# Splitting a sequence's attention jobs at a unit boundary, and storing the last result by halves

## The chip, the cores and the metric

The kernel runs on one core of one Trainium2 chip. The metric is the device time of the whole kernel in microseconds. Five engines run side by side, each in its own program order: TensorE (PE, with its weight loads shown as PEld), VectorE (DVE), ScalarE (ACT), GpSimd (POOL) and SyncE (SP), which issues most of the DMA transfers.

## The reference

```
scores = q @ k^T / 8;  ret = scores * gamma_h ** (i - j) for i >= j, else 0
x = (ret @ v), heads side by side            # 8 sequences of 576 tokens, 8 heads of 64 -> 4608 x 512
xn = x / sqrt(mean(x*x) + 1e-6) * rms_g
out = (silu(xn @ w_gate) * (xn @ w_val)) @ w_out     # 512 -> 1536 -> 512
```

Everything is float32, except that gate's, value's and the output's weights arrive as 64-bit floats and are brought to 32 bits in the kernel.

## The kernel before

**Attention.** A job is one sequence `b` and one pair of heads `hp`, so there are 8 x 4 = 32 jobs, numbered in that order. A job has nine chunks of 64 tokens (`NC` = 9, `L` = 64). Within a chunk the product is taken directly (`scores`, then `weigh` by the decay and the causal mask, then `values`), and what earlier chunks hand on goes through a running 64 x 64 state per head (`states` on PE, `sums` on DVE, `carried` on PE). The moves at the end of `carried` (L397, DVE) put the result into the token-feature tile `x`. One call of `slot(j)` issues `values(j-1)`, `scores(j)`, `states(j)`, `weigh(j)`, `carried(j-1)` and `sums(j)`. `carried` may start only after a small write to `tick` that follows `values`.

**Units.** The feed-forward part takes 12 units of 384 tokens (`U`; `HU` = 192 is half). Three units cover two sequences: units 0 and 1 hold all 576 tokens of the first sequence and the first 192 of the second; unit 2 is the other 384 tokens of the second.

**Opening.** Units 0 and 1 are treated apart. First all eight jobs of the first two sequences run, one `slot` after the other. Their q and k are turned by matmuls against an identity (`turn`, evicted by ACT, L239 and L248), and their v is scaled by ACT (`scale_v`, L264). Between slots DVE and ACT begin to round the weights: there are 18 chunks of 64-bit weights, and each takes the DVE operations L811 (exponent), L838, L843 (mantissa), L848 (sign) and L856 (join), with three ACT operations L827 between L811 and L848. The words of a chunk are loaded into one of four places, and a load that waits for a place is issued from ACT's queue right behind the L848 which frees it (L795).

**Gate's and value's products of units 0 and 1** (`up_plain`, L614) follow. They are issued in 48 equal steps: for each of three groups of columns, gate (m = 0) and then value (m = 1), for each of two units, four steps. I number these steps 0 to 47; steps 24 to 31 and 40 to 47 are value's in the second and third group. One step is four matmuls of 128x384 into one PSUM bank, followed by its eviction: ACT with a silu for gate (L622), DVE with a multiplication for value (L620). After each step the program queues two more pieces of weight rounding (`weights(2)`) and one ACT piece (`act(1)`). PE's results of steps, `values`, the last state of a job (`last`) and the turned q and k all come from one pool of five PSUM banks.

**After that** the output products of units 1 and 0 run (`across`, L688), while DVE combines the weights (L652, L672), and units 2 to 11 follow in one steady form, in which products are formed from sums and differences of blocks (L557, L564). Here the remaining jobs, from number 8 on, are spread over the units: `load_next` fetches q, k and v by DMA two jobs ahead, `prepare` turns q and k by DVE transposes (L255), and `slot` runs the job between two products.

The order on each engine is the program's (`manual_schedule`), so an instruction that waits holds up all that is queued behind it on its engine.

Of the kernel before, what the change touches and what calls it, by code (L numbers as in the profile page):

```python
# [14 lines left out]
P = 128  # L15
# [26 lines left out]
def kernel(  # L42
# [88 lines left out]
    jobs = [(b, hp) for b in range(B) for hp in range(NHP)]  # L131
# [4 lines left out]

    def load_qk(j):
        b, hp = jobs[j]
        for nm, src in (("q", q), ("k", k)):

            t = raw.tile([P, S // SQ, SQ], F32, tag=nm + "raw", name=f"{nm}raw_{j}")
            for e in range(2):
                rows = src[b, 2 * hp + e].rearrange("(t b) (i a) -> i b t a", b=SQ, a=SQ)
                for i in range(D // SQ):
                    r = e * D + i * SQ
                    nc.sync.dma_start(out=t[r : r + SQ], in_=rows[i])
            st[j][nm + "raw"] = t

    def load_first(j, tails):

        b, hp = jobs[j]
        d = st[j]
        room = h_of[0].rearrange("p f t -> p (f t)")
        part = room[:, j * 4 * P : j * 4 * P + 4 * P]
        d["q"] = part.rearrange("p (e t d) -> p e t d", e=2, d=D)
        nc.sync.dma_start(
            out=part.rearrange("p (e t) -> p e t", e=2),
            in_=q[b, 2 * hp : 2 * hp + 2, : NFULL * P].rearrange("e (p t) d -> p e (t d)", p=P),  # L160
        )
        for nm, src in (("k", k), ("v", v)):
            t = d[nm] = first_places[nm][j].rearrange("p (c e d) -> p c e d", e=2, d=D)
            for e in range(2):
                nc.sync.dma_start(
                    out=t[:, :, e],
                    in_=src[b, 2 * hp + e, : NFULL * P].rearrange("(c p) d -> p c d", p=P),
                )
            for n in (0, 1) if nm == "k" else (2,):
                load_tails(b, n, tails)  # L170
# [33 lines left out]
    def load_kv(j):  # L204

        b, hp = jobs[j]
        for nm, src, bufs in (("k", k, 4), ("v", v, 3)):
            t = raw.tile([P, NFULL, 2, D], F32, tag=nm, name=f"{nm}_{j}", bufs=bufs)
            for e in range(2):
                nc.sync.dma_start(  # L210
                    out=t[:, :, e],
                    in_=src[b, 2 * hp + e, : NFULL * P].rearrange("(c p) d -> p c d", p=P),
                )
            st[j][nm] = t
        t = st[j]["vt"] = raw.tile([L, 2, D], F32, tag="vt", name=f"vt_{j}", bufs=3)
        nc.sync.dma_start(
            out=t, in_=v[b, 2 * hp : 2 * hp + 2, NFULL * P :].rearrange("e p d -> p e d")
        )

    def turn(j):  # L220

        d = st[j]
        last = bank(f"turn_{j}_t")
        for nm in "qk":
            ps = bank(f"turn_{j}_{nm}")
            for c in range(NFULL):
                if nm == "k":
                    nc.tensor.transpose(
                        out=ps[:, c * P : c * P + P],
                        in_=d["k"][:, c].rearrange("p e d -> p (e d)"), identity=ident,  # L230
                    )
                    continue
                for e in range(2):
                    nc.tensor.matmul(
                        ps[side(e), c::NFULL], lhsT=d["q"][:, e, c], rhs=ident,
                        start=True, stop=True,
                    )
            t = d[nm + "T"] = att.tile([P, S], F32, tag=nm + "T", name=f"{nm}T_{j}")
            nc.scalar.copy(out=t[:, : NFULL * P], in_=ps)  # L239
        for i, nm in enumerate("qk"):  # L240
            o = slice(i * TAIL, i * TAIL + TAIL)
            nc.tensor.transpose(
                out=last[:, o], in_=d[nm + "t"].rearrange("p e d -> p (e d)"),
                identity=ident[:TAIL, :TAIL],
            )
        for i, nm in enumerate("qk"):
            o = slice(i * TAIL, i * TAIL + TAIL)
            nc.scalar.copy(out=d[nm + "T"][:, NFULL * P :], in_=last[:, o])  # L248

    def prepare(j):  # L250

        d = st[j]
        for nm in ("q", "k"):
            t = att.tile([P, S], F32, tag=nm + "T", name=f"{nm}T_{j}")
            nc.vector.transpose(out=t, in_=d.pop(nm + "raw").rearrange("p t a -> p (t a)"))  # L255
            d[nm + "T"] = t
        scale_v(j)

    def scale_v(j):
        d = st[j]  # L260
        hp = jobs[j][1]
        for e in range(2):
            for t in (d["v"][:, :, e], d["vt"][:, e]):
                nc.scalar.activation(  # L264
                    out=t, in_=t, func=AF.Copy, scale=gv[: t.shape[0], hp, e : e + 1]
                )
# [9 lines left out]
    def scores(j):  # L276

        d = st[j]
        s = d["s"] = trio.tile([P, 3, 512], F32, tag="s", name=f"s_{j}")
        for c in range(NC + 1):  # L280
            i, odd = divmod(c, 2)
            c = min(c, NC - 1)
            for e in range(2):
                nc.tensor.matmul(  # L284
                    s[side(odd), e, i * L : i * L + L], lhsT=d["kT"][side(e), c * L : c * L + L],
                    rhs=d["qT"][side(e), c * L : c * L + L], start=True, stop=True,
                )
# [8 lines left out]
    def states(j):  # L296

        d = st[j]
        d["last"] = bank(f"last_{j}")
        for c in range(NC - 1):  # L300
# [8 lines left out]
    def weigh(j):  # L309

        d = st[j]
        hp = jobs[j][1]
        s = d["s"]
        ret = d["ret"] = att.tile([P, 2, NFULL + 1, L], F32, tag="ret", name=f"ret_{j}", bufs=1)
        for e in range(2):
            nc.vector.scalar_tensor_tensor(
                out=ret[:, e], in0=s[:, e, :SC].rearrange("p (c k) -> p c k", k=L),
                scalar=float(_gamma(H)[2 * hp + e] ** -L),
                in1=causal.unsqueeze(1).to_broadcast([P, NFULL + 1, L]),
# [3 lines left out]
    def sums(j):  # L323

        d = st[j]
        hp = jobs[j][1]
        t = d["sum"] = att.tile([P, NC - 1, L], F32, tag="sum", name=f"sum_{j}")
        for c in range(NC - 1):
            part = state_of(d, c)
            if c == 0:  # L330
                nc.vector.tensor_copy(out=t[:, 0], in_=part)
                continue
            nc.vector.scalar_tensor_tensor(  # L333
                out=t[:, c], in0=t[:, c - 1], scalar=gc[:, hp : hp + 1], in1=part,
                op0=ALU.mult, op1=ALU.add,
            )
        del d["s"], d["last"]
# [10 lines left out]
    def values(j):  # L348

        d = st[j]  # L350
        av = d["av"] = [bank(f"av_{j}_{i}") for i in range(2)]
        for c in range(NC):
            i, odd = divmod(c, 2)
            for e in range(2):
# [4 lines left out]
                    start=(c < 2), stop=False, skip_group_check=True,  # L359
# [3 lines left out]
        if j == 2 * NHP:  # L363
# [5 lines left out]
    def carried(j):  # L369

        d = st[j]
        b, hp = jobs[j]
        av = d["av"]
        for c in range(1, NC):
            i, odd = divmod(c, 2)
            for e in range(2):
                mm = nc.tensor.matmul(  # L377
                    av[odd][column(j, odd, e), i * L : i * L + L], lhsT=d["sum"][side(e), c - 1],
                    rhs=d["qT"][side(e), c * L : c * L + L],
                    start=False, stop=(c >= NC - 2), skip_group_check=True,  # L380
                )
                if c == 1 and e == 0:
                    follow(mm, d["valued"])
        for c0, c1 in ((0, 2 * HU), (2 * HU, S)) if b % 2 == 0 else ((0, HU), (HU, S)):
# [289 lines left out]
    def across(u):  # L674
# [8 lines left out]
        def product(rhs, ps, start):  # L683
            k = 7 * (u - 2) + n_done
            a = first_blocks[ORDER[n_done]] if u < 2 else w_slots[:, k % 4]
            for i in range(2):
                for c in range(NH):
# [4 lines left out]
                    )  # L692
            if u > 1 and n_done < 3:
# [8 lines left out]
        def result(row, col, a, ps):  # L702
# [5 lines left out]
            end = u == NU - 1  # L708
            if not end:
                nc.vector.transpose(out=o, in_=r)  # L710
            o_of = o.rearrange("p (d t r) -> p d t r", d=2, r=SQ)
            for d in range(2):
                if end:
                    half = slice(d * HU, d * HU + HU)
                    nc.vector.transpose(out=o[:, half], in_=r[:, half])
                for i in range(P // SQ):
                    c0 = row * DH + d * P + i * SQ
                    t0 = u * U + col * HU
                    queue = nc.scalar if end and i % 2 else nc.sync
                    queue.dma_start(  # L720
                        out=out[t0 : t0 + HU, c0 : c0 + SQ].rearrange("(t c) r -> c t r", c=SQ),
                        in_=o_of[i * SQ : i * SQ + SQ, d],
                    )
# [31 lines left out]
        product(b21, w, False)  # L755
        result(1, 0, u2, w)
# [134 lines left out]
    steps = rounding()  # L891

# [12 lines left out]
    def start():  # L905
# [20 lines left out]
        for j in range(2 * NHP):  # L926
            load_first(j, {0: range(2), 1: range(2, H), NHP: range(H)}.get(j))
# [9 lines left out]
        squares = []  # L937
        for j in range(2 * NHP):
# [24 lines left out]
        made = combine_out()  # L963
        for m, g in [(m, g) for g in range(NG) for m in range(2)]:
            for u in range(2):
                weights_to(4 * g + 2 * m + 1)
                for i, _ in enumerate(up_plain(u, m, g)):
                    if not (u or m or g):
# [23 lines left out]
        following(2 * NHP - 1)  # L992
# [12 lines left out]
        slot(8, rest=False)  # L1005
        following(8)
# [3 lines left out]
        slot(9)  # L1010
        following(9)
# [7 lines left out]
    def behind(u, i):  # L1019
        at, n = SLOTS[u % 3]  # L1020
        if i in at:
            j = u // 3 * 8 + n + at.index(i)
# [7 lines left out]
    with tc.manual_schedule():  # L1030
# [4 lines left out]
        for u in range(2, NU):  # L1035
# [11 lines left out]
            for i, _ in enumerate(rest):  # L1047
                if i == 0 and turns:
                    prepare_next(turns.pop())
                if i == 2:  # L1050
                    behind(u, 6)
                    at, n = SLOTS[u % 3]
                    if 2 * NG - 1 in at:
                        load_next(u // 3 * 8 + n + len(at) - 1)
# [31 lines left out]
```

## Time and profile before

| what | value |
|---|---|
| median of 3 runs | 1143.16 us (1141.73 to 1143.99) |
| span of the profiled run | 1141.5 us |
| PE busy | 1119.3 us, 98% |
| DVE busy | 726.9 us, 64% |
| ACT busy | 258.7 us, 23% |
| granted TensorE clock, mean | 0.995 |
| opening, until the first gate product | 0 to 61.7 us |
| the 48 steps | 61.7 to 191.0 us |
| output products of units 1 and 0 | 191.0 to 248.3 us |

A busy PE in this table is one that has an instruction running; the stage decides whether that instruction waits for anything. The stages are read from the chain of waits, which lists in order of time the pieces of work that the end of the run goes back to.

### The profile page before, as it was taken

What the parts mean: (1) busy time and instruction counts of PE and PEld (TensorE: products, weight loads), DVE (VectorE), ACT (ScalarE), POOL (GpSimd) and SP (SyncE); (2) the same over time, 40 slices, a digit from 0 to 9 for tenths busy, and PEclk for the clock granted to TensorE, in tenths of its full rate; (3) what the DMA queues carried; (4) which work ended last, traced back from release to release, by engine and by line L of the source; (5) the groups of instructions that cost most, each with busy time, mean ns of one, the idle gap of its engine ahead of it and who ended that gap; (6) DMA issues with size and microseconds to landing.
All of it is one profiled execution on the core that took longest, in us unless ns stands there. A gap on an engine that the chain in (4) does not pass through costs nothing.

```text
span 1141.5 us, 24713 instructions
## 1 busy us (share of the span) xinstructions
PE 1119.3 (98%) x10470; PEld 1046.5 (92%) x10470; DVE 726.9 (64%) x1431; ACT 258.7 (23%) x508; POOL 39.5 (3%) x64
## 2 busy tenths in 40 slices
PE   8889999999999999999999999999999999999998
PEld 6655557999999999999999999999999999999998
DVE  5788877745685685375767676466577566446352
ACT  5545642002211221111221121121121220120210
POOL 0000000370000000000000000000000000000000
PEclk8999999999999999999999999999999999999999
DMA  8765326335463465044444555306436403303304
GB/s 205 208 157 175 113 102 211 62 67 127 110 131 76 139 149 155 1 109 100 100 125 67 122 140 121 115 30 121 107 89 143 131 32 96 127 1 99 124 1 111
DMA packets 292943, 125.40 MB, mean 110 GB/s; under 512 B 270433, under 2 KB 275809, under 8 KB 292833
## 3 DMA queue, kind: packets, MB, share of 16 engines
q1 hardware_dynamic: 282688, 107.66, 38.3%
q10 hardware_dynamic: 10144, 16.16, 4.4%
q8 instruction: 82, 1.34, 0.5%
q14 instruction: 29, 0.23, 0.1%
HBM read 108.83 MB, written 14.94 MB: 108 GB/s over the span
## 4 chain that ended last, share of the span: by engine, by line
PE 93%; DVE 3%; issue 1%; DMA 1%; ACT 1%; SPq 0%; DVEq 0%; POOLq 0%; POOL 0%; ACTq 0%
PE w L557 13%; PE x L557 13%; PE z L557 13%; PE up L614 11%; PE xo L688 8%; PE wo L688 8%; PE zo L688 8%; PE y L557 6%; PE yo L688 4%; PE av L355 2%; PE av L377 2%; PE s L284 2%; PE s L304 1%; DVE x L397 1%; DVE sum L333 1%
## 5 line engine op out<-in xcount | busy, mean ns | idle before, releaser
L581 ACT COPY m<-x 128x384 f32<-128x384 f32 x60 | 28.7, 478 | 338.3 <-PE x L557 338.3
L688 PE MATMUL xo<-h,w_out 128*128 128x192 f32 x528 | 90.3, 328 | 0.0
L557 PE MATMUL w<-sums,w_val 128*128 128x192 f32 x480 | 88.6, 328 | 0.4
L557 PE MATMUL x<-x,w_val 128*128 128x192 f32 x480 | 88.8, 328 | 0.0
L557 PE MATMUL z<-x,w_gate 128*128 128x192 f32 x480 | 87.9, 326 | 0.7 <-DVE u L564 0.7
L557 PE MATMUL x<-x,w_gate 128*128 128x192 f32 x480 | 88.5, 328 | 0.0
L557 PE MATMUL w<-sums,w_gate 128*128 128x192 f32 x480 | 87.8, 326 | 0.0
L557 PE MATMUL z<-x,w_val 128*128 128x192 f32 x480 | 87.8, 326 | 0.0
L688 PEld LDWEIGHTS xo<-h,w_out 128*128 128x128 f32 x528 | 85.9, 190 | 0.6
L688 PE MATMUL wo<-h,w_out 128*128 128x192 f32 x504 | 85.3, 326 | 0.0
L564 DVE TENSOR_TENSOR u<-m,y 128x384 f32<-128x384 f32 x60 | 33.1, 552 | 79.1 <-PE y L557 79.1
L688 PEld LDWEIGHTS wo<-h,w_out 128*128 128x128 f32 x504 | 82.5, 190 | 0.0
L557 PEld LDWEIGHTS w<-sums,w_val 128*128 128x128 f32 x480 | 79.2, 190 | 2.7 <-DVE c L564 2.7
L557 PEld LDWEIGHTS z<-x,w_gate 128*128 128x128 f32 x480 | 79.6, 190 | 1.0 <-issue 1.0
L557 PEld LDWEIGHTS x<-x,w_val 128*128 128x128 f32 x480 | 79.2, 190 | 0.6
L557 PEld LDWEIGHTS x<-x,w_gate 128*128 128x128 f32 x480 | 79.3, 190 | 0.5
L557 PEld LDWEIGHTS z<-x,w_val 128*128 128x128 f32 x480 | 79.7, 190 | 0.0
L557 PEld LDWEIGHTS w<-sums,w_gate 128*128 128x128 f32 x480 | 79.6, 190 | 0.0
L564 DVE TENSOR_TENSOR h<-u,w 128x384 f32<-128x384 f32 x60 | 33.0, 550 | 69.5 <-PE w L557 69.4
L576 ACT ACTIVATE h<-h 128x384 f32<-128x384 f32 x90 | 47.0, 523 | 89.5 <-DVE h L564 89.5
L614 PE MATMUL up<-x,w_gate 128*128 128x384 f32 x192 | 63.3, 488 | 0.9 <-DVE x L526 0.7
L614 PE MATMUL up<-x,w_val 128*128 128x384 f32 x192 | 62.7, 487 | 0.0
(187 smaller groups left out, 1770.6 us busy)
## 6 DMA issues: line engine op xcount, KB each, us to landing
w_out<-w_blocks SPq DMA_DIRECT2D x70, 768.0 KB, 5.1
out_dram<-o SPq DMA_DIRECT2D x368, 24.0 KB, 1.6
qraw<-in_q_dram SPq DMA_DIRECT2D x96, 72.0 KB, 2.9
kraw<-in_k_dram SPq DMA_DIRECT2D x96, 72.0 KB, 3.0
k<-in_k_dram SPq DMA_DIRECT2D x48, 128.0 KB, 3.0
v<-in_v_dram SPq DMA_DIRECT2D x48, 128.0 KB, 3.1
w_out<-in_moe_w_gate_dram ACTq DMA_DIRECT2D x5, 1024.0 KB, 5.9
w_out<-in_moe_w_out_dram ACTq DMA_DIRECT2D x3, 1024.0 KB, 4.9
```

The source lines that it names most:

```text
L284: nc.tensor.matmul(s[side(odd), e, i * L : i * L + L], lhsT=d["kT"][side(e), c * L : c * L + L], rhs=d["qT"][side(e), c * L : c * L + L], ...
L304: nc.tensor.matmul(o[side(e)], lhsT=d["k"][side(odd), i, e], rhs=d["v"][side(odd), i, e], start=True, stop=True,)
L333: nc.vector.scalar_tensor_tensor(out=t[:, c], in0=t[:, c - 1], scalar=gc[:, hp : hp + 1], in1=part, op0=ALU.mult, op1=ALU.add,)
L355: mm = nc.tensor.matmul(av[odd][column(j, odd, e), i * L : i * L + L], lhsT=d["v"][side(odd), i, e] if c < NC - 1 else d["vt"][:, e], rhs= ...
L377: mm = nc.tensor.matmul(av[odd][column(j, odd, e), i * L : i * L + L], lhsT=d["sum"][side(e), c - 1], rhs=d["qT"][side(e), c * L : c * L + L],
L397: nc.vector.tensor_tensor(out=x[to, first - c0 // L :: 2], in0=av[odd][at, i * L : (i + n) * L].rearrange("p (c k) -> p c k", k=L), in1=g. ...
L557: nc.tensor.matmul(ps[:, i * HU : i * HU + HU], lhsT=w_up[m][:, 2 * blk + c, cut], rhs=t_of[u][blk][:, c], start=(start and i == c == 0), ...
L564: nc.vector.tensor_tensor(out=o, in0=a, in1=pairs_of(ps), op=ALU.add)
L576: nc.scalar.activation(out=o, in_=c, func=AF.Silu)
L581: nc.scalar.copy(out=s1, in_=pairs_of(x_))
L614: nc.tensor.matmul(ps[:, :U], lhsT=w_up[m][:, 4 * half + c, i * P : i * P + P], rhs=x_of[u][:, c], start=(c == 0), stop=(c == NHP - 1),)
L688: nc.tensor.matmul(ps[:, i * HU : i * HU + HU], lhsT=a[:, c, i * P : i * P + P], rhs=rhs[:, c], start=(start and i == c == 0), stop=False, ...
```

## The change

The jobs of the second sequence are cut at its token 192, where unit 2 begins. Only the first three chunks of those four jobs stay in the opening, since units 0 and 1 need no more. The other six chunks become four jobs of their own (numbers 8 to 11), which are loaded, prepared and run among the 48 steps of gate's and value's products. The state that a first part hands to its second part is kept in unit 2's tile `x`, in a place that the second part overwrites last. All later jobs keep their places and get numbers that are four higher.

Two smaller things change besides. The transposes of the third later job (`prepare`) are no longer queued right before unit 2, but within its first block of products. And the last result of the last unit is made by halves: once the first half's products are done, its sum, transpose and stores are issued, and the second half's products follow; before, one sum was taken over both halves after all products.

```diff
-    jobs = [(b, hp) for b in range(B) for hp in range(NHP)]
+    CUT = HU // L
+    parts = [(0, 0, NC), (1, 0, CUT), (1, CUT, NC)] + [(b, 0, NC) for b in range(2, B)]
+    jobs = [(b, hp, c0, c1) for b, c0, c1 in parts for hp in range(NHP)]
+    LATER_JOBS = 3 * NHP
...
+    LATER_AT = (29, 33, 37, 41, 45)
...
+        def later(step):
+
+            if step == LATER_AT[0] - 8:
+                following(2 * NHP - 1)
+            elif step in LATER_AT:
+                j = 2 * NHP + LATER_AT.index(step)
+                if j < LATER_JOBS:
+                    slot(j, rest=(j > 2 * NHP))
+                    if j + 1 < LATER_JOBS:
+                        following(j)
+                else:
+                    values(j - 1)
+                    carried(j - 1)
...
                 for i, _ in enumerate(up_plain(u, m, g)):
+                    step += 1
+                    later(step)
...
         combine(0)
-        slot(9)
-        following(9)
+        slot(LATER_JOBS + 1)
+        load_next(LATER_JOBS + 1)
+        turns.append(LATER_JOBS + 1)
...
+        def last_result(d):
+
+            if not d:
+                o = outs.tile([P, DM], F32, tag="o", name="o_last")
+                halves.extend((temp("c_last"), o))
+            r, o = halves
+            nc.vector.tensor_tensor(
+                out=r[:, half(d)], in0=u2[:, half(d)], in1=w[:, half(d)], op=ALU.add
+            )
+            nc.vector.transpose(out=o[:, half(d)], in_=r[:, half(d)])
+            store(o, 1, 0, d)
...
-        product(b21, w, False)
-        result(1, 0, u2, w)
+        if u == NU - 1:
+            product(b21, w, False, last_result)
+        else:
+            product(b21, w, False)
+            result(1, 0, u2, w)
```

`following(j)` is `prepare(j + 1)` and the load of job `j + 2`. So at step 21 job 8 is prepared and job 9 loaded; at steps 29, 33, 37 and 41 the slots of jobs 8 to 11 run, each with the next one's preparation but for the last; at step 45 `values` and `carried` of job 11 close the series. The rest of the diff carries the bounds of a job's chunks through loads, turns, scores, states, sums and moves.

## The prediction

> **What bounds the kernel now.** I read the page, then the chain of waits, stage by stage, then the timelines of DVE, ACT and the weight loads where the moved work will land. All times are us; step s is the s-th of the 48 product steps.
>
> ```profile
> PE   8889999999999999999999999999999999999998
> DVE  5788877745685685375767676466577566446352
> ```
>
> Of the page's 40 slices (28.5 us each) only the first three leave PE idle; everything later is PE work. So the opening can lose idle time, and what is moved into the steps is paid for at PE's price.
>
> The chain of waits in the opening, from the fifth job's slot on:
>
> ```profile
> 41.31 0.93 PE av L355 x36
> 42.23 0.58 PE s L284 x40
> ...
> 44.02 0.93 PE av L377 x31
> 44.95 1.05 PE turn_q L234 x16
> 46.02 0.59 ACT qT L239
> 46.61 0.58 ACT kT L239
> ...
> 58.90 2.18 issue
> ...
> 61.70 2.78 PE up L614 x8
> ...
> 76.88 100.89 PE up L614 x312
> ```
>
> A slot is a ring of PE work and two ACT evictions, about 5.2 long, with stretches called issue in between (0.89, 2.06, 0.40, 0.81 and 2.18 from 30.8 on). DVE is nearly as long. Its timeline in the slots of jobs 4 to 7 has 0.89 for weighing, 2.35 for the sums, 0.95 for the moves, and 0.55 to 2.2 for squares, norm and weight rounding each. Step 0 starts at 61.70, step 4 at 76.88, and then a step is 8 x 0.324 = 2.59 until 190.97 without a gap.
>
> In the steps, the end of the weight rounding on DVE:
>
> ```profile
> 169.25 1.22 DVE L848 SCALAR_TENSOR_TENSOR w_gate<-w_gate 128x1024 uint32<-128x1024 uint32 x1
> 175.50 0.70 DVE L811 TENSOR_SCALAR w_gate<-w_gate 128x1024 uint32<-128x1024 uint32 x1 [5.03 <-DMA w_gate<-in_moe_w_out_dram]
> ...
> 180.24 1.23 DVE L848 SCALAR_TENSOR_TENSOR w_gate<-w_gate 128x1024 uint32<-128x1024 uint32 x1 [1.04 <-ACT w_gate L827]
> 181.39 0.54 DVE L620 TENSOR_TENSOR h<-h,up 128x384 f32<-128x384 f32 x1
> ```
>
> The L848 of chunk 16 frees the place of chunk 17, whose load takes 5.0; the L811 of chunk 17 waits for it, and the evictions are queued behind. The L620 at 181.39 evicts step 40, which PE ended at 76.88 + 37 x 2.59 = 172.8, 8.6 earlier. ACT is held in the same way:
>
> ```profile
> 176.23 1.15 ACT L827 ACTIVATE w_gate<-w_gate,least 128x1024 f32<-128x1024 uint32 x1 [9.01 <-DVE w_gate L811]
> 177.28 0.47 ACT L622 ACTIVATE w_val<-up 128x384 f32<-128x384 f32 x1
> ```
>
> That L622 evicts step 38. And the weight loads:
>
> ```profile
> 177.80 12.55 PEld L614 LDWEIGHTS up<-x,w_val 128*128 128x128 f32 x40 [0.65 <-ACT w_val L622]
> ```
>
> Step 43 takes the bank of step 38, five back: PE already runs its five banks out here and waits for nothing only because it is just in time.
>
> [...]queue q8 has 82 packets and 1.34 MB, 16.3 KB each, and PE resumes after the issue stretches at 31.7, 37.9, 43.3 and 49.6, some 126 matmuls (252 instructions) apart. [...]So loads of the moved jobs delay chunk loads; in the opening, where both run, a chunk takes 5.9 in the median against 4.9 for the w_out chunks on ACT's queue. [...]weighing, which needs the scores alone, starts after the states in neighbouring columns (DVE ret L316 waits for PE s L304). [...]
>
> **The change part by part.**
>
> *Opening.* Up to the turn of job 4 (30.1) nothing changes. DVE is busy without a break to the L811 at 33.99 to 34.69, so the weighing of job 4 starts at 34.7 (before: 35.7). From there DVE sets the pace. A half slot costs it 2 x 0.245 for weighing 128 columns (0.445 for 320, at 1.05 ns a column by 0.55 for 384 and 1.22 for 1024), 0.21 + 2 x 0.31 for sums and 0.29 + 0.21 for two moves instead of four: 1.83 against 4.2. Slot 4 still moves job 3 (0.94) and has two squares (1.1) and L838 (0.69): to 38.8. Slot 5: 1.83, r 0.16, L843 1.22, then it waits for the power on POOL (1.65) and forms the diagonals (0.68): to 43.3. Slot 6: 1.83, norm 2.19, L848 1.22: to 48.6. Slot 7: 1.83 and two squares 1.2: to 51.65. PE, about 2.2 a half slot, stays beside this[...]. Step 0 begins when the first norm column is there, at 45.9, ends at 48.5, waits for the weighing of job 7 (49.1), and its moves end at 52.15, against 67.63. Square and sum 1.1, L811 0.69 and L856 1.22 follow, to 55.1; before, 69.99. Step 2 needs that L856, so all later steps are **14.9 earlier**.
>
> *PE's work in the steps.* Full slots in units 2 and 3 take 0.67 values, 0.58 scores, 0.39 states, 0.50 carried and 0.2 of switching. Of that 6/9, 8/10, 5/8 and 6/8: 1.7 for a later job. Five calls, 0.7 + 3 x 1.7 + 1.2 (the last with nothing to hide tick), are 7.0.
>
> *DVE's work in the steps.* A later job costs 0.76 weighing, 5 x 0.31 sums, 1.07 moves (0.35 and 2 x 0.36), 1.10 transposes (0.77 and 0.735 for 576 columns, less 192 x 1.05 ns each). I follow chunk 17's L811, before at 175.50:
> - Step 29 puts 3.4 (no moves yet) ahead of chunk 13's L848. DVE has 0.16 idle there: +3.3, and the load behind it is later by as much.
> - Step 33 puts 4.5 between chunk 14's L848 and the next L811, where DVE idled 3.9 for a load: +0.6.
> - Step 37 puts 4.5 ahead of chunk 16's L848, whose load everything waits for: +4.5.
> - The loads of jobs 10 and 12 are issued beside two of those chunk loads. By 5.9 against 4.9 I take +0.6 each, +1.2; nothing at best, 1.5 each at worst.
>
> Together +9.6 (8.4 to 11.4): L811 at 185.1 on the old clock. Queued behind it, and thus late: on ACT the evictions of steps 38 and 39, on DVE those of 40 to 43. PE waits for their banks. The slot at step 41 takes three banks (two av, one last), so step 42 now needs step 40's bank. Before, step 45 did. From L811 to the end of that eviction is 181.9 - 175.5 = 6.4; then steps 42 to 47 (6 x 2.59) and the last call (1.2): the steps end 23.2 after L811, against 191.0 - 175.5 = 15.5 before. So **+7.7 + 9.6 = 17.3**; 7.0 of it is PE's own work and the rest waiting. An earlier wait at step 35 (about 3, ACT held by the load behind chunk 14's L848) lies inside this. The transposes at step 21 cost nothing: by step 27 DVE waited 0.52 for PE before. ACT's v scaling, tick's memset on POOL and the load of job 8 lie beside PE's products.
>
> *Unit 2.* PE waits 0.70 at 257.2 for a DVE sum behind the transposes; with these queued later: **-0.7**.
>
> *The end.* Before: sum 0.57, two half transposes, four stores of 0.43 per queue, the last issued at 1138.8. After: sum 0.35, transpose 0.33, two stores per queue, 1.1 sooner. If PE may not write the bank meanwhile, it waits about 0.5 for the first half's sum: **-0.8** (0.6 to 1.1).
>
> Sum: -14.9 + 17.3 - 0.7 - 0.8 = +0.9; 1143.16 + 0.9 = **1144.1**.
>
> **The rivals.**
> - *Hidden.* The jobs' DVE work falls into DVE's 13.4 of waiting (3.4, 3.9, 5.0 and 1.0 from 150 to 180), and PE pays 7.0 and a wait of some 4: -14.9 + 11 - 1.5 = -5.4, 1137.8; with no wait 1133.8. For it: the idle time is there. Against it: two of the three insertions before L811 come just before an L848 that starts a load, so the idle time moves with them.
> - *More contention.* Chunk loads at the worst value (+1.8), and the opening 3 less[...]: 1144.1 + 4.8 = 1148.9, slower. For it: DMA is 79% busy from 30 to 62. Against it: DVE, not DMA, set the pace there.
>
> **How the numbers follow.** An even trade (1141 to 1147): 0.48. Hidden (1133 to 1141): 0.31. Contention (1147 to 1153): 0.21. The bound of 0.2% is 2.3, so faster means under 1140.9, slower over 1145.4. The even trade is spread over that bound: 0.02 of it faster, 0.34 same, 0.12 slower. So faster 0.33, same 0.34, slower 0.33. The range cuts off 1 in 10 at each end: 1136.0 to 1149.5.
>
> **What would show it.** Step 0 near 46 and step 4 near 62 (opening); a wait of several us at the weight loads or av of the slot at step 41 and at step 42, for ACT w_val L622 and DVE h L620; chunk 17's L811 some 9.6 later against step 31 than before; steps ending near 193.4. If PE runs through steps 35 to 47 with waits under 3 in all, I am wrong and Hidden is right; if step 4 starts after 65, the opening's sum is wrong.

## The result and the profile after

| | before | after |
|---|---|---|
| median of 6 runs each | 1141.89 us (1139.81 to 1143.99) | 1148.47 us (1146.38 to 1149.55) |
| ratio after / before | | 1.0056, 95% interval 1.0041 to 1.0072 |
| span of the profiled run | 1141.5 us | 1147.0 us |
| step 4 starts | 76.88 | 62.47 |
| exponent of chunk 17 starts | 175.50 | 172.72 |
| the steps end | 190.97 | 198.91 |

The change makes the kernel slower, by 6.6 us in the medians and 5.5 in the profiled pair. The forecast was 0.9 slower. The median lies in the band that the forecast gave to *More contention*, not in that of its even trade.

In the new numbering of lines the product steps are L652, their evictions L660 (ACT) and L658 (DVE). Of the weight rounding, the exponent is L871, the sign L908, ACT's operations L887, and the load behind the sign L855. `weigh` is L342, the moves L435, the transposes of `prepare` L272, `values` L390, `carried` L412 and the write to `tick` L401.

The page's slices of the changed kernel, the ones shown of before:

```profile
PE   7899988999999999999999999999999999999998
DVE  5888777747586586466766776466577576446353
```

The third slice reads 9 where it read 8, and step 4 starts 14.4 sooner: the opening did get shorter. The sixth and seventh slice, from 143 to 201 us, fell from 9 to 8: PE now waits there. Which waits these are, the chain of waits shows. From step 4 on it reads (start, length, what):

```profile
62.47 67.35 PE up L652 x208
...
130.75 0.76 DVE ret L342 x2
...
136.29 1.15 DVE w_gate L908
137.46 6.60 DMA w_out<-in_moe_w_out_dram
144.16 0.69 DVE w_gate L871
...
147.85 0.67 DVE ret L342 x2
148.53 0.36 DVE x L435
...
149.40 9.67 PE up L652 x24
...
164.63 1.12 DVE w_gate L908
165.78 6.92 DMA w_gate<-in_moe_w_out_dram
172.72 0.70 DVE w_gate L871
...
179.20 12.95 PE up L652 x32
```

Before, PE's products were one piece of 100.89 from step 4 on. Now the chain leaves PE at step 29 (129.8) and goes through DVE: weighing, the sign of chunk 13, the load which that sign releases, the exponent of chunk 15, weighing again, and back to PE for one stretch; then the same once more through chunks 16 and 17. The loop that the forecast describes, slot to sign to load to exponent to eviction, is there line by line. PE's three longest waits between 62 and 200 (us in total, times, longest):

```profile
PE up L652 <- DVE x L435: 3.6, 1, 3.6
PE av L390 <- ACT w_val L660: 3.5, 1, 3.5
PE up L652 <- DVE h L658: 1.3, 1, 1.3
```

The first is step 35, whose bank waits for slot 9's moves; the second is the slot of step 41, the third step 42. These are the places and the releasers of the forecast. DVE's and ACT's timelines around chunk 17:

```profile
164.56 1.18 DVE L908 SCALAR_TENSOR_TENSOR w_gate<-w_gate 128x1024 uint32<-128x1024 uint32 x1
172.72 0.69 DVE L871 TENSOR_SCALAR w_gate<-w_gate 128x1024 uint32<-128x1024 uint32 x1 [6.98 <-DMA w_gate<-in_moe_w_out_dram]
```

```profile
173.45 1.15 ACT L887 ACTIVATE w_gate<-w_gate,least 128x1024 f32<-128x1024 uint32 x1 [10.58 <-DVE w_gate L871]
174.50 0.47 ACT L660 ACTIVATE w_val<-up 128x384 f32<-128x384 f32 x1
```

DVE idles 6.98 for chunk 17 (5.03 before), and ACT 10.58 behind it (9.01). The L660 at 174.50 is the eviction that the slot of step 41 waits for.

What the forecast doesn't have is in the windows around the two long pauses, of step 35 and step 41 (us, busy time and count of PE, PEld, DVE, ACT, POOL, then the granted clock, the DMA share and GB/s):

```profile
151.00:153.00 2.00, 2.00 (x5) 1.09 (x4) 2.00 (x4) 2.00 (x3) 0.00 (x0) 0.50 0.71 250
173.00:175.00 2.00, 0.00 (x0) 0.00 (x0) 2.00 (x3) 1.55 (x3) 0.00 (x0) 0.69 1.23 208
175.00:177.00 2.00, 1.98 (x72) 1.98 (x76) 1.38 (x2) 2.00 (x3) 0.09 (x1) 0.50 0.91 260
181.00:183.00 2.00, 2.00 (x4) 1.00 (x3) 1.91 (x7) 0.00 (x0) 0.00 (x0) 0.50 0.75 253
185.00:187.00 2.00, 2.00 (x8) 1.21 (x7) 0.00 (x1) 0.00 (x0) 0.00 (x0) 1.00 0.00 0
```

From the pause of step 41 on, PE runs at half its clock until about 184: four matmuls in 2 us, where the row of 185 has eight. A weight load of step 42 comes every 0.64 instead of 0.32. The pause of step 35 does the same from 149.9 to 153.3, so that steps 35 to 37 take 9.67 (the row of 149.40 above) instead of 3 x 2.59 = 7.78. Of that 1.9 little reaches the exponent of chunk 17: VectorE waits only 0.33 for the scores that come next (160.35).

### The profile page after: what moved, and what is told of

The parts are those of the page before. It is cut to its first block, busy times and chain, and to the rows that moved or that the text cites. A ratio compares the mean times of both kernels' runs of the same rounds, so it can differ in the third digit from the quotient of the medians.

```text
span 1147.0 us, 24779 instructions
## 1 busy us (share of the span) xinstructions
PE 1121.7 (98%) x10454; PEld 1045.3 (91%) x10454; DVE 733.4 (64%) x1452; ACT 257.8 (22%) x508; POOL 40.1 (4%) x68
## 4 chain that ended last, share of the span: by engine, by line
PE 93%; DVE 3%; DMA 2%; ACT 1%; issue 1%; SPq 0%; POOL 0%; DVEq 0%; POOLq 0%; ACTq 0%
PE x L595 14%; PE w L595 14%; PE z L595 14%; PE up L652 9%; PE xo L726 8%; PE wo L726 8%; PE zo L726 8%; PE y L595 7%; PE yo L726 4%; PE av L390 2%; PE av L412 2%; PE s L307 1%; PE s L329 1%; DMA w_gate<-in_moe_w_out_dram 1%; DMA w_out<-in_moe_w_out_dram 1%
## 5 line engine op out<-in xcount | busy, mean ns | idle before, releaser
L652 PE MATMUL up<-x,w_gate 128*128 128x384 f32 x192 | 65.8, 499 | 4.9 <-DVE x L435 3.6
L652 PE MATMUL up<-x,w_val 128*128 128x384 f32 x192 | 65.6, 501 | 1.3 <-DVE h L658 1.3
```

Source lines behind the costliest of these rows:

```text
L652: nc.tensor.matmul(ps[:, :U], lhsT=w_up[m][:, 4 * half + c, i * P : i * P + P], rhs=x_of[u][:, c], start=(c == 0), stop=(c == NHP - 1),)
```

## The experiments

Two theories stood against each other. **Chain**: the price is paid in waits. VectorE's queue sets the exponent of chunk 17, the five banks set what follows it, and where the slots stand in that queue decides the price. **Price**: TensorE's own work for the moved slots and the half clock pay for the opening, wherever the slots stand. Times behind the exponent are counted to the first weight load of the output products (`xo`), which lies 25.7 behind it in the changed kernel and 15.0 before.

**1. One piece of weight work before each slot and one after it, where the slots stand ahead of both.**

```diff
                     step += 1
-                    later(step)
...
-                    weights(2)
+                    weights(1)
+                    later(step)
+                    weights(1)
```

> The same as the changed kernel, but in each step the slot is queued between the step's two pieces of weight rounding instead of ahead of both. Theory Chain (the weight rounding with its loads, held up on DVE by the inserted work, sets the end of the steps through PE's five banks): at step 37 the sign of chunk 16 and the load of chunk 17 now come before the slot's 4.5 us of DVE work, which then lies in the load's time. Chunk 17's exponent, 110.25 us after step 4 began, comes some 4.6 us sooner, at 105 to 106; the steps end at least 4.6 us sooner (up to 7, if PE's pauses get too short for the clock to drop), so 1141 to 1144 us. Theory Price (the steps are longer by PE's own work on the moved jobs and by loads that share the DMA engines; where the work stands in DVE's order does not matter): 1148 us, within 1.

Measured: 1142.47, ratio to before 1.0009 (1.0000 to 1.0018). Exponent of chunk 17 at step 4 + 105.68, against + 110.25 in the changed kernel; steps 129.0 instead of 136.0 (to the first `xo` weight load). Slot 10 now stands behind the sign of chunk 16 and no longer ahead of it, so its load starts without waiting for it. PE's waits:

```profile
PE up L652 <- DVE x L435: 3.9, 1, 3.9
PE up L652 <- DVE h L658: 0.6, 1, 0.6
```

The waits of steps 41 and 42, 4.8 together, are down to 0.6; that of step 35 stays. No matmul was taken out, so this speaks for Chain. Of the 4.6 by which the exponent of chunk 17 comes sooner, the sign of chunk 16 gives 2.7 (it now waits for ACT instead). The other 1.9 is chunk 17's load, 4.70 from the end of its issue to the exponent instead of 6.57: the loads of job 12 moved back with the slot and no longer run beside it.

**2. Slot 11 later, where all evictions have caught up.**

```diff
-    LATER_AT = (29, 33, 37, 41, 45)
+    LATER_AT = (29, 33, 37, 44, 47)
```

> The same as the changed kernel, but the slot of job 11 comes at step 44 instead of 41, and the closing values and carried at step 47 instead of 45. Theory Chain: chunk 17's exponent stays 110.2 us after step 4 (within 0.5), but the slot no longer takes three banks while the evictions of steps 38 to 41 wait behind that chunk. PE waits at step 43 for the eviction of step 38 instead of at the slot, and the steps end about 19 us after the exponent instead of 26.2: about 7 us faster in all, 1141 to 1143 us. Theory Price: the same work in another place, 1148 us within 1.

Measured: 1142.34, ratio 1.0013 (1.0004 to 1.0022). Exponent at + 110.36, as in the changed kernel, and 19.0 from there to the end, against 25.7: 6.7 less. Both the banks and the half clock after the pause go with it. PE's waits:

```profile
PE up L652 <- DVE x L435: 3.8, 1, 3.8
PE av L412 <- POOL tick L401: 0.3, 1, 0.3
PE up L652 <- ACT w_val L660: 0.2, 1, 0.2
```

**3. The loads of jobs 10 and 12 made to follow the exponents of chunks 15 and 17.**

```diff
+                    if j in (10, 12) and nm == "q" and e == i == 0:
+                        follow(dma, exp_ins[{10: 15, 12: 17}[j]])
...
+    LOADS_AT = {32: 8, 38: 10}
...
+            if step in LOADS_AT:
+                load_next(LOADS_AT[step])
```

For this the loads of these two jobs are also issued later in the program, at steps 32 and 38.

> The same as the changed kernel, but the loads of jobs 10 and 12 start only after the exponents of chunks 15 and 17, so that these two chunk loads have the DMA engines to themselves. If sharing made these chunk loads longer (6.7 and 6.9 us instead of 5.1 and 5.0), chunk 17's exponent comes up to 3.5 us sooner, at 106.7 to 107.5 us after step 4, and the steps end as much sooner: 1144 to 1146 us. If not, the loads keep their times and the total is 1148 us within 1.

Measured: 1150.07 in four runs, ratio 1.0070 (1.0054 to 1.0086). From the end of their issue to the exponent, the loads of chunks 15 and 17 took 4.70 and 4.62 before, 6.32 and 6.57 in the changed kernel, and 4.62 and 4.61 here. So the job's transfers beside them did lengthen them, by 3.6 together. But nothing was gained: the transposes of job 10 now wait 3.3 for its k, the sign of a chunk 2.1 for ACT, and the exponent of chunk 17 comes at + 111.7. The cost is confirmed, this cure is not.

**4. Five products without use before the slot of step 41, to keep TensorE's clock up.**

```diff
+                    if j == LATER_JOBS - 1:
+                        hot = trio.tile([P, 3, 512], F32, tag="s", name="hot")
+                        for _ in range(5):
+                            nc.tensor.matmul(
+                                hot[:, 0, :U], lhsT=ones, rhs=x_of[1][:, 0], start=True, stop=True
+                            )
```

> The same as the changed kernel, with five further matmuls of 128x384 on PE ahead of the slot at step 41, whose result nobody reads; they fill 3.2 us of the 3.5 us for which PE waits there for a bank. If the half clock in step 42 (eight matmul records of 0.64 us instead of 0.32) comes from PE's pause, it is gone: the slot and step 42 run at full clock, and the steps end about 2.6 us sooner, 1145 to 1146 us, though PE has more to do. If the clock has another cause, or the pause isn't what matters, the time is 1148 us or more by up to 3.

Measured: 1148.66, ratio 1.0061 (1.0046 to 1.0076). The row of 181 to 183 that had the half clock:

```profile
181.00:183.00 2.00, 2.00 (x8) 1.21 (x7) 1.97 (x6) 0.00 (x0) 0.00 (x0) 1.00 0.33 95
```

Full clock, and the stretch behind the exponent is 23.35 instead of 25.71, although step 42 now waits 2.1 instead of 1.3. So the half clock of this second pause cost 2.4 there, the longer wait deducted. The time did not follow: in this profile the opening was 1.6 longer and the stretch from unit 2 to the last product 1.5 longer, and the median is that of the changed kernel. Four runs don't tell whether those two belong to the edit.

**5. Edits 1 and 2 together**, and once more for a second profile.

> Both edits at once: one unit of weight work before each slot and one after it, and slot 11 at step 44 with the closing at step 47. Chain (VectorE's queue sets chunk 17's exponent, the five banks set what follows it): the two gains are in different stretches and add. Exponent of chunk 17 at step 4 + 105.7 as with the first edit alone, and 19 from there to the first xo weight load as with the second alone: the steps take 124 to 126, against 136.4 in the changed kernel and 114.1 before. Time 1135.5 to 1138, 4 to 6 under the kernel before. Price (TensorE's own work for the slots and half clock pay for the opening): each edit alone has reached the kernel before and no more is to be had: 1141 to 1143.

Measured: 1142.97, ratio 1.0005 (0.9993 to 1.0016), with a profiled run at the low end (1139.8). The exponent came at + 103.9 and the steps took 126.8 to the first `xo` weight load.

> The kernel with both edits unchanged, for a second profile: its first profiled run took 1139.8, 3.2 under its median of 1143.0, so the profile did not show what the typical run does. Opening theory (PE's issue stretches[...] vary from run to run): step 4 between 62 and 66, later than 62.4 by as much as the run is longer than 1139.8, and the steps again 126.5 to 127.5. Steps theory (chunk loads and the waits behind them vary): step 4 near 62.4, and the steps 128 to 131 with a longer wait at step 35 or 42.

Measured: 1142.67, ratio 1.0006 (0.9991 to 1.0021). Step 4 at 63.8, exponent at + 105.9, steps 128.7: both parts of the run had grown. So the gains did not add, against what Chain said, and the steps are only 0.3 and 2.2 shorter than with the better of the two alone. The reason can be read in the waits of experiment 1: with the exponent 4.6 sooner, step 42 waits only 0.6, so the second edit had almost nothing left to remove. Both edits cure the same wait. What stays in both profiles is step 35, with 3.3 and 4.0.

**6. As 5, and slot 8 at step 30**, where its VectorE work stands behind the sign of chunk 13; and once more.

```diff
-    LATER_AT = (29, 33, 37, 44, 47)
+    LATER_AT = (30, 33, 37, 44, 47)
```

> As the run with both edits, and slot 8 one step later, at step 30, where its 3.4 of VectorE work stands behind chunk 13's sign op and not ahead of it, so that it falls into the wait for chunk 15's load (4.6 idle at 140.4 with the first edit alone). Chain: chunk 13's sign op and all behind it 3.3 sooner, exponent of chunk 17 at step 4 + 102 to 103, steps 121 to 123, time 1132 to 1135. Price: slot 8 costs TensorE the same at either step: no difference to the run with both edits within 1.0.

Measured: 1137.54, ratio 0.9962 (0.9949 to 0.9976). VectorE's timeline where slot 8 and the load of chunk 15 meet:

```profile
131.87 1.22 DVE L908 SCALAR_TENSOR_TENSOR w_gate<-w_out,w_gate 128x1024 uint32<-128x1024 uint32 x1
133.00 0.75 DVE L342 SCALAR_TENSOR_TENSOR ret<-s,causal 128x256 f32<-128x256 f32 x2
...
138.51 0.70 DVE L871 TENSOR_SCALAR w_gate<-w_out 128x1024 uint32<-128x1024 uint32 x1 [0.71 <-DMA w_out<-in_moe_w_out_dram]
```

The sign comes first, its load runs while DVE does slot 8, and of the 5.0 idle only 0.71 is left. The exponent of chunk 17 is at + 100.7, the steps take 122.4, and PE waits 0.6 in all between 120 and 200:

```profile
PE av L412 <- POOL tick L401: 0.3, 1, 0.3
PE up L652 <- DVE x L435: 0.3, 1, 0.3
```

The profiled run is the fastest of its 13 (1135.0), as was that of the first profile of experiment 5. One step's difference in place, with PE's work the same, brings the exponent 3.2 forward and takes 5.4 off the median. Price can't explain that. The second time:

> The kernel with slot 8 at step 30 unchanged, for a second profile and more runs. Median 1137 to 1138 again. Opening theory: step 4 later than 61.4 by as much as the run is longer than 1135.0, steps 122 to 123. Steps theory: step 4 near 61.4, steps 124 to 126.

Measured: 1140.19, ratio 0.9973 (0.9960 to 0.9986). Its 21 runs lie in two groups, 10 at 1135.8 to 1138.4 and 11 at 1140.2 to 1141.6, and the profiled one (1141.2) is from the upper. The median therefore falls just into the upper group: it is 2.5 below that of experiment 5's second time, and 1.0 below that of the kernel before in the same set, where the first set had 4.4. There step 35 waits 3.3 again: the load of chunk 15 took 8.1 from its issue to the exponent, against 5.0 in the first profile. Neither theory of the expectation alone holds: step 4 was 1.8 later, and the steps were 4.7 longer.

**7. The last result by halves as the only edit to the kernel before.**

> The kernel before, with the last result by halves as the only edit. Both theories: TensorE waits some 0.44 for the first half's sum in the middle of the last product, and the stores end 0.5 to 1.1 sooner counted from the start of the last product: the tail of 9.08 becomes 8.0 to 8.6. Time 0.5 to 1.1 under the kernel before, which the interval may or may not tell from nothing; the steps and the opening stay as before (step 4 at 76.9, steps 114.1).

Measured: 1141.85, ratio 0.9996 (0.9986 to 1.0006). From the start of the last product to the end 8.61, against 9.08 before: 0.47 sooner, and in the time it can't be told from nothing. But the opening, which is the same code as before, had step 4 at 73.0. So:

**8. The kernel before once more.**

> The kernel before unchanged, for another profile of its opening: 76.9 in the first profile, 73.0 in the run with the last result by halves alone, which is the same up to there. Opening theory: step 4 anywhere from 73 to 77, and the steps 113.6 to 113.7 to the first xo weight load whatever the time of the run. Steps theory: step 4 near 76.9 and the steps vary by a us or more.

Measured: 1140.93. Step 4 at 74.6, steps 113.5. PE's stretches called issue between 28 and 77 sum to 6.3, 3.1 and 4.6 in the three profiles with step 4 at 76.9, 73.0 and 74.6. The opening varies with them; the steps of the kernel before don't. The clock adds to it: the slower two profiles each have one stretch of 3.4 at half clock in their slots (from 50.4 and from 38.5), and the fastest has none.

**9. Experiment 6, with the loads of jobs 10, 11 and 12 made to follow the exponents of chunks 15, 16 and 17.**

```diff
+                    if j in (10, 11, 12) and nm == "q" and e == i == 0:
+                        follow(dma, exp_ins[j + 5])
...
+    LOADS_AT = {32: 8, 35: 9, 38: 10}
```

As in experiment 3 these loads are also issued later. Chunks 15 and 17 then have no job's load beside them; chunk 16 has that of job 10.

> The kernel with slot 8 at step 30, and the loads of jobs 10, 11 and 12 made to follow the exponents of chunks 15, 16 and 17, so that none of them runs beside a chunk's load. In the two profiles of that kernel the load of chunk 15 took 5.0 and 8.1 from its issue to its exponent, and its runs fall into two groups, 1135.0 to 1138.4 and 1139.3 to 1141.6. Contention theory (the job's small packets and the chunk's share the DMA engines, in an order that varies): loads of chunks 15 and 17 4.6 to 5.1 as before, no wait over 0.5 at step 35, steps 121 to 123, one group of runs, median 1135 to 1137.5. Price theory (TensorE's own work and the opening vary): two groups again, median 1137.5 to 1140.

Measured: 1139.65, ratio 0.9985 (0.9977 to 0.9993): no more gained than without the edit. Two waits came in the place of the gain, 5.4 of ACT for a job's v and 1.6 of DVE for a k. And the load of chunk 15 took 6.5, with no job's packets beside it. The DMA view of that stretch, 136 to 143 (GB/s in 40 slices, then the queues):

```profile
GB/s 94 0 0 0 94 94 140 23 23 140 304 304 374 398 398 492 398 374 421 374 398 398 351 211 47 0 23 23 23 23 23 47 23 23 23 0 0 0 0 0
...
q10 hardware_dynamic: 272, 1.05, 46.6%
q8 instruction: 1, 0.02, 1.0%
```

The chunk is 1.05 MB in packets of 4 KB; at 140.2 all but some ten are there, and the rest arrives one by one, at 23 GB/s. Why they come so late is not shown. The only other traffic is a packet of instructions, 0.2 behind the load's issue. The long load of experiment 6's second profile has one too, 0.8 behind it, and a tail of the same kind. So sharing with the job's packets isn't the whole cause.

**10. Experiment 6, with 40 products of 64x64 without use** behind a norm in step 1, meant to have a packet of instructions land elsewhere against the load of chunk 15.

> The kernel with slot 8 at step 30 and its job loads as they were, and 40 products of 64 by 64 without use behind the first norm of unit 1, where TensorE waits about 1.0 for VectorE. They cost nothing themselves[...]. In the two profiles with the long load of chunk 15 (last packet 8.8 and 7.4 after its issue, 90 in 100 of the packets there by 5.4) one instruction packet of 16 KB landed 1.2 to 1.7 after the issue; in the other loads it landed before the issue or over 5 behind it, and the last packet 5.3 to 6.9 after. Fetch theory: [...]last packet of chunk 15 5.3 to 6.0 after its issue, exponent of chunk 17 at step 4 + 100 to 102, steps 121.5 to 123.5, and the runs in one group, within 4 of each other. Contention theory (only the job's packets): the load of chunk 15 and the runs vary as before, in two groups over 6 apart. The opening may shift by 1 or 2 either way[...].

Measured: 1142.80, ratio 1.0016 (1.0008 to 1.0024). The 40 products were not free: they ran as 80 of 0.061, 4.88 in a wait of 1.0, and step 4 came at 67.4. After that all went as the fetch theory said: 5.3 from the issue to the exponent of chunk 15, exponent of chunk 17 at + 100.6, steps 122.7, and 19 of 21 runs within 3.5. But in the first profile of experiment 6, whose load is short (5.0), an instruction packet lies 0.15 behind the issue, within 0.1 of its place in experiment 9, whose load is long (6.5). What makes a load long is not shown.

## Why the forecast was right in most of its steps and 5 short

| step | forecast | measured |
|---|---|---|
| opening (step 4) | -14.9 | -14.4 |
| exponent of chunk 17 later, by step 29 | +3.3 | +3.3 |
| by step 33 | +0.6 | +0.2 |
| by step 37 | +4.5 | +4.6 |
| by loads that share the DMA | +1.2 | +3.6 |
| exponent to the end of the steps | +7.7 | +10.7 |
| unit 2 to the last product | -0.7 | -1.9 |
| end | -0.8 | -0.5 |
| sum | +0.9 | +5.5 |

The measured column is the pair of profiles; 1147.0 - 1141.5 = 5.5, and its rows are rounded.

*Opening.* Right in that pair, where the chain runs mostly through DVE from 39 to 55 as forecast, and step 0 began at 47.9 instead of 46. (The terms printed for slot 4 add up to 39.3, not 38.8, and those for slot 5 to 43.1, not 43.3; both slips are small.) But the step 4 it starts from lies at 76.9, 74.6 and 73.0 in three profiles (mean 74.8), and at 61.4 to 64.3, mean 63.0, in ten of the changed kernel and of variants with the same opening. The typical gain is nearer 11.8: part of what I counted was the issue time of one run, and that the pair shows 14.4 is partly luck.

*VectorE's queue.* The three insertions cost what they were forecast to, to 0.4. The mis-sized term here is the load sharing: 0.6 for each of two loads, measured 1.62 and 1.94, above the 1.5 that I gave for the worst. I had taken it from the opening's loads, 5.9 against 4.9. Experiment 3 shows the cause by its absence: 4.62 and 4.61 without the job's transfers.

*The banks.* The mechanism is right, with PE's waits at the slot of step 41 and at step 42, for the two releasers named. Experiment 2 takes it away and 6.7 goes. What was missing from the sum is the clock: the pause of 3.5 brought TensorE to half its clock, at a cost of some 2.4 by experiment 4. In the trace it is 0.50 from 2.3 into the pause of 3.5 until, behind the second wait, 4.7 of products had run again. Pauses of 3.0 and 3.3 (experiments 4 and 5) brought the half clock as well. I had counted the wait and not what follows it.

*The same time counted on PE.* From step 4 to the first `xo` product the changed kernel takes 22.4 more than the kernel before: 8.7 of waits, 7.1 for the slots' own work at full clock (taken from experiment 6; the forecast had 7.0), and 5.7 more for products and slots than in experiment 6, whose clock stays full. The rest is 0.8. The forecast had 17.3, with 10.3 of waiting. So on PE's side the waits were not too small in the sum; the half clock behind both pauses was put at nothing.

*Unit 2 and the end.* The wait of 0.70 is gone as forecast; another 1.2 wasn't foreseen, and most of it is issue time (0.34 and 0.74 in the profile before, at 272 and 293) that the profile after lacks there. At the end PE waits 0.44 in the middle for the first half's sum, as guessed.

*The rivals.* Hidden fell: PE waits 8.4 at steps 35, 41 and 42. It fell by the places of the slots, not through the idea. With the slots up to three steps elsewhere and between two pieces of weight work (the first profile of experiment 6), the waits come to 0.6, the steps cost 122.4 - 113.6 = 8.8 more (7.1 of it PE's work for the slots), and the kernel is faster than before, by 0.4% and 0.3% in two sets of runs. More contention named about the right time, partly by luck. Of its two causes the first came, and the loads got longer still than it had them. The opening gained the forecast 14.9 but for 0.5 in the profiled pair; where it typically gains 3 less, 2.1 of that is the slow opening of the profile that I counted from. And the half clock was missing there too.

*Open.* What makes the last packets of a chunk load come one by one (at 23 GB/s in experiment 9), and why the loads of experiment 6 vary from run to run at all, are open.

## What to carry to other kernels

When work is moved into a stretch where TensorE is busy, what counts is its place in the queues of the engines that feed it: put it behind the operation that releases the next transfer, where it fills the wait, and not ahead of it, where it delays the transfer and then waits as well (slot 8 one step later took 5.4 us off the median, experiment 6 against 5). Count the buffers that a moved piece takes at the point where their evictions are furthest behind (experiment 2: 6.7 us). Before two cures are added up, ask whether they remove the same wait (experiment 5). And where a wait of TensorE gets as long as the one of 3.5 us here, count the half clock behind it too (2.4 us by experiment 4).

## What the runs showed of the hardware that was not expected

- Pauses of TensorE of 3.0 to 4.0 us in this stretch were followed by half its clock: in the changed kernel (3.6 and 3.5), in experiments 1 (3.9), 2 (3.8), 4 (3.0) and 5 (3.3 and 4.0) and in 6's second profile (3.3). Pauses of 2.1 and 1.8 that stood alone (experiments 4 and 9) were not. In the changed kernel the half clock lasted 3.4 us behind the pause of step 35 (149.9 to 153.3) and 10.2 behind that of step 41 (173.8 to 184.0). The second cost 2.4 more than the pause itself (experiment 4); in the first PE lost 1.9, which was almost hidden because VectorE was the later one.
- A 1 MB load in 4 KB packets took 4.5 to 4.8 from the end of its issue to its use when alone (chunks 15 and 17). Beside a job's loads in rows of 128 and 256 bytes it took 5.0 and 5.3 when they were issued 2.3 behind it (experiments 6 and 10), 5.2 to 6.3 in other profiles (experiments 1, 2, 4 and 5, and the changed kernel's chunk 15, beside 0.2 MB), and 6.5 and 6.6 at most (experiments 2 and 4, and the changed kernel's chunk 17, beside 0.3 MB). Two more took 6.5 and 8.1 when a last dozen packets came one by one.
- In the opening of the kernel before, PE resumes from its stretches called issue at 31.7, 37.9, 43.3, 49.6 and 61.1, some 126 matmuls apart and 254 before the last. These stretches sum to 6.3, 3.1 and 4.6 in three profiles of one and the same code.
